# A table of ninety-two task priorities in a self-scheduled attention and gated feed-forward kernel

## Chip, cores and metric

The kernel runs on one core of a Trainium2 chip. The metric is the device time of one execution in microseconds, median of the runs. The profile describes one execution; its span, from the first to the last instruction on the core, is 276.8 us, and the run that it was taken from lasted 278.56 us.

## What is computed

Attention for 4 batches, 8 heads, 768 positions and a head dimension of 64, followed by a gated feed-forward layer over the 3072 resulting rows of width 512. Heads 0, 2 and 6 ("retrieval") attend to all earlier positions; the others attend to the first 4 positions ("sinks") and a window of 64.

```python
causal = rel >= 0
stream_keep = causal & (is_sink | ((rel >= 0) & (rel < 64)))
mask = where(is_retrieval, causal, stream_keep)
a = softmax(where(mask, q @ k.T / 8, -1e9))
x = (a @ v)                      # -> (3072, 512), heads side by side

g, val = x @ w_gate, x @ w_val   # (512, 1536) each
ffn = (gelu(g) * val) @ w_out    # (1536, 512)
out = x + sigmoid(x @ w_res) * ffn
```

## The kernel before

The Python program builds a graph of 1670 tasks (360 of them are dummy matmuls, see below), runs a list scheduler over that graph when the program is built, and emits each engine's instructions in the order that the scheduler found. On the chip nothing is scheduled any more: each engine executes its list in order and waits on semaphores where a task depends on another engine.

The 3072 rows are taken in six chunks of four tiles of 128 rows. In chunk c the tasks are, with the source line that the profile shows and the engine in brackets:

- `qkT`, `qkE`: q and k turned so that the head dimension lies on partitions (chunks 0 and 1), L631 [PE] and L646 [ACT or DVE]; later chunks use transposing DMAs, L669.
- `sc`: scores, q against k, L768 [PE]; `sk`: scores against the sinks, L856 [PE]; `exp`, L784 and L863 [ACT]; `mask`, L820 [DVE].
- `win`, `av`, `avk`: the weights times v, by window, by whole tiles and for the sinks, L885, L895, L909 [PE]; `rcp`, `norm16`, `norm`: division by the sums, L935, L946, L948 [DVE].
- `xT`, `xE`: the result turned, L963 [PE], and copied out of PSUM, L970 [ACT or DVE].
- `g`, `v`: gate and value matmuls, L988 [PE], in halves of two 512-column matmuls; there are 12 pairs f = 0..11 in a chunk. `gelu`, L1000 [ACT]; `h`, their product, L1002 [DVE].
- `res`: the residual gate, L1016 [PE], with `tanh`, L1019 [ACT]; `ff`: the output matmuls, L1031 [PE], in pieces of two; `gated` and `add`, L1035 and L1038 [DVE]; `out`, the store, L1041.
- `warm`: dummy matmuls on a blank tile, L1047 [PE], priority 1e9, so that they run when nothing else can; those that are left are dropped when the first gate matmul is placed.

Scores use half of the array's rows for each of two heads, window products half of its columns, sink scores a quarter of its rows and columns; the scheduler calls this the task's mode (`row`, `col`, `quarter`, or none for the whole array).

The part that picks the next task, with cuts:

```python
ENGS = ("pe", "act", "dve", "pool", "sp")
SWITCH = 0.1
LAT = {"pe": 0.20, "act": 0.10, "dve": 0.08, "pool": 0.12, "sp": 0.1}

def schedule(self):
    ...
    while left:
        for e in ENGS:
            if free[e] > now:
                continue
            best = bkey = None
            for t in cand[e]:
                if t.boost and all(x.end is not None and x.end <= now for x in t.boost[0]):
                    t.prio, t.boost = t.boost[1], None
                key = (int(e == "pe" and mode is not None and t.mode != mode), t.prio, t.seq)
                if t.ready > now or (best is not None and key >= bkey):
                    continue
                ...                      # a task with two possible engines; are its buffers free?
                if ok:
                    best, bkey = t, key
            ...
            dur = t.dur
            if e == "act" and t.fset and t.fset != fset:
                dur += 1.3
            if e == "pe":
                dur += SWITCH if t.mode != mode else 0.0
            free[e] = now + dur
            ...
```

So a task is a candidate once its producers are done by the scheduler's own clock. Among candidates the lowest `prio` wins, except that the tensor engine first takes one of the mode that it is in. Priorities before are given by a rule: they begin at 1000 times the chunk, with gate and value at +500, the outputs at +2400 + 10 per tile:

```python
pr = 1000 * c + 500 + f           # gate and value matmuls, gelu, product
...
if c0 == 0 and c > 0:             # their first halves are wanted late until all of xT is there
    for t in (tg, tv):
        t.boost, t.prio = ([t_ for _, t_ in xttoks], pr), 1000 * c + 1499
...
pr = 1000 * c + 2400 + 10 * lt    # res, tanh, ff, gated, add, store
...
P.pr = 1000 * c + 40 * k_         # scores of the k_-th pair of heads; sinks 1000 * c + 45
```

Two fixed order rules remain whatever the priorities are: gate and value tasks of a chunk come after all its scores (and, but for the first f, after all its `xT`), and the scores of chunk c + 1 come after the gate and value tasks of f = 10 of chunk c and after its `xT`.

PSUM has eight banks, and the kinds of task share them with caps: two score buffers of two banks each (banks 2 to 5), one pair of banks (0, 1) for the products with v, up to four banks at once out of 2 to 7 for gate and value, banks 6 and 7 for the outputs.

```python
"av2": (1, [(0, 1)]), "sc": (2, [(2, 3), (4, 5)]),
"gv": (4, one(6, 7, 5, 4, 3, 2)), "gv00": (2, one(6, 7)), "out": (2, one(6, 7)), ...
```

Of the kernel before, what the change touches and what calls it, by code (L numbers as in the profile page):

```python
# [36 lines left out]
ROWS_UNTIL = 2  # L37

VK = ((1, 4), (3, 4), (4, 5), (4, 7))

class Task:
    __slots__ = ("eng", "dur", "fn", "deps", "order", "prio", "bufs", "fset", "dma",
# [387 lines left out]
def build_kernel(nc, q, k, v, w_gate, w_val, w_out, w_res, out):  # L430
    assert N_SINK <= 64 and WINDOW == 64
    G = Graph(nc)
# [37 lines left out]
    def at(buf):  # L470
        if buf.pool is P_ps:
            return psum[:, buf.slot[0] * 512:(buf.slot[-1] + 1) * 512]
        return buf.pool.items[buf.slot]
# [68 lines left out]
    def batch(b):  # L542
        if b not in batches:
            B_ = B()
            B_.v, B_.vs, B_.vk, B_.qkt = Buf(P_v), Buf(P_vs), Buf(P_vk), Buf(P_qkt)
            B_.vtok, B_.vstok, B_.qtok, B_.ktok = {}, {}, {}, {}
            batches[b] = B_
        return batches[b]

    def values(b, a, z, base, each, on_engines=False):  # L550
# [6 lines left out]
        if a == 0:  # L557

            def vk(on, j, h0, h1):
                def fn(e):  # L560
                    o = at(BB.vk)[32 * j:32 * j + N_SINK, 2 * j:2 * j + 2, :]
                    i_ = at(BB.v)[0:N_SINK, 0, h0:h1 + 1:h1 - h0, :]
                    return e.activation(out=o, in_=i_, func=AF.Copy) if on == "act" else e.tensor_copy(out=o, in_=i_)
                return fn
            BB.vktok = [G.flex({"dve": (0.3, vk("dve", j, *hs)), "act": (0.35, vk("act", j, *hs))},
                               [BB.vtok[0]], base + 1500, bufs=[BB.v, BB.vk], name="vk") for j, hs in enumerate(VK)]
            for t in BB.vktok:
# [301 lines left out]
    def weigh(P, tiles, sinks, xbuf, x16, xtoks, xdeps, last):  # L869
# [30 lines left out]
        def sinkf(x, h):  # L900
            def fn(e):
                r = []
                for lt, (b, i) in enumerate(tiles):
# [3 lines left out]
                    j = sinks.four[b, i] if h == 4 else (1, 3, 5, 7).index(h)  # L907
                    sl = 2 * j + VK[j].index(h)
                    r.append(e.matmul(at(av)[:, o:o + 65], lhsT=at(sinks.et)[:, ko:ko + 128], rhs=at(batch(b).vk)[:, sl, :],  # L909
# [157 lines left out]
    for c in range(len(CHUNKS)):  # L1067
# [9 lines left out]
        for t in ph(c + 1, "exp"):  # L1077
            t.order += gelu[NF - 1:]

    span = G.schedule()  # L1080
    G.assign_waits()
    G.emit()
# [3 lines left out]
def bass_duo_attention_split__then__geglu_gated_residual_kernel(  # L1086
    nc: bass.Bass,
    q: bass.AP,
    k: bass.AP,
    v: bass.AP,  # L1090
    is_retrieval: bass.AP,
    n_sink: bass.AP,
    window: bass.AP,
    moe_w_gate: bass.AP,
    moe_w_val: bass.AP,
    moe_w_out: bass.AP,
    moe_w_res: bass.AP,
    out: bass.AP,
):
    assert int(n_sink) == N_SINK and int(window) == WINDOW  # L1100
    build_kernel(nc, q, k, v, moe_w_gate, moe_w_val, moe_w_out, moe_w_res, out)
# [33 lines left out]
```

The softmax here doesn't subtract the row's maximum and nothing guards it: scores larger than these inputs give would overflow.

## Time and profile before

| | before |
|---|---|
| median of 3 runs | 278.73 us (278.38 to 278.83) |
| span of the profiled execution | 276.8 us |
| PE matmul busy | 270.3 us, 98% |
| DVE, ACT, POOL busy | 143.0, 137.5, 86.2 us |
| bytes read from HBM, written | 29.36 MB, 6.29 MB |
| dummy matmuls executed (L1047) | 151, all before 22.0 us |

How to read it: matmuls overlap one another in the records. One of 512 columns is listed with 379 ns although the next may start 216 ns after it, so a busy PE is not a PE at its peak. Time that PE loses therefore shows in the distance from one matmul's start to the next one's, and in dummy matmuls, which count as busy, rather than in the busy share. In the chain of work that ended last, each row is a start, a length and a run of instructions of one line.

### The profile page before, as it was taken

To read this page: it belongs to the slowest core of one execution; us is meant where nothing else is said; L and a number is where in the kernel's file an instruction comes from. 1 tells how busy PE (TensorE), PEld (TensorE's weight loads), DVE (VectorE), ACT (ScalarE), POOL (GpSimd) and SP (SyncE) were. 2 spreads that over 40 slices of the span, in tenths; PEclk is the share of its full clock that TensorE was granted. 3 is DMA by queue.
4 is the path that set the end of the run, shared out by engine and by line. 5 is a ranking of instruction groups with operands and counts; after the bars stand their busy time and mean duration, and the time that the engine had idled before them with its cause. 6 is when DMAs were issued, how large, how long until landed. Compare 5 with 4: busy or idle time off the path is not lost.

```text
span 276.8 us, 5687 instructions
## 1 busy us (share of the span) xinstructions
PE 270.3 (98%) x2407; PEld 138.9 (50%) x2407; DVE 143.0 (52%) x260; ACT 137.5 (50%) x199; POOL 86.2 (31%) x120
## 2 busy tenths in 40 slices
PE   7999999999899999999999999999999999999995
PEld 7775454455444456444455444456444455544443
DVE  2696342477433467534377533366633258633234
ACT  3655366673433966334773333766233777333210
POOL 8999249991491613991000000000000000000000
PEclk9999999999999999999999999999999999999999
DMA  6999999999999999999711100021100011200022
GB/s 88 165 203 207 185 206 177 151 194 133 176 131 154 247 138 201 158 155 125 191 41 73 44 0 2 0 76 41 40 0 0 2 41 38 78 2 0 0 76 78
DMA packets 92474, 27.81 MB, mean 100 GB/s; under 512 B 81184, under 2 KB 88864, under 8 KB 92448
## 3 DMA queue, kind: packets, MB, share of 16 engines
q0 software_dynamic: 70320, 14.69, 66.8%
q1 hardware_dynamic: 22128, 12.76, 23.7%
q8 instruction: 19, 0.31, 0.5%
q14 instruction: 7, 0.06, 0.1%
HBM read 29.36 MB, written 6.29 MB: 129 GB/s over the span
## 4 chain that ended last, share of the span: by engine, by line
PE 95%; DVE 2%; DMA 2%; issue 1%; ACT 0%; POOLq 0%
PE ps L988 45%; PE ps L1031 23%; PE ps L1016 7%; PE ps L768 5%; PE ps L895 3%; PE ps L1047 3%; PE ps L885 2%; PE ps L963 2%; PE ps L631 2%; DMA qks<-in_q_dram 2%; PE ps L909 1%; PE ps L856 1%; ACT xT L970 0%; DVE otile L1035 0%; DVE x L946 0%
## 5 line engine op out<-in xcount | busy, mean ns | idle before, releaser
L1002 DVE SCALAR_TENSOR_TENSOR hT<-gact,ps 128x512 f16<-128x512 f16 x72 | 49.5, 687 | 70.5 <-ACT gact L1000 70.5
L988 PE MATMUL ps<-xT,wg 128*128 128x512 f16 x288 | 85.2, 379 | 0.5 <-ACT xT L970 0.5
L988 PE MATMUL ps<-xT,wv 128*128 128x512 f16 x288 | 85.2, 379 | 0.0
L1000 ACT ACTIVATE gact<-ps 128x512 f16<-128x512 f32 x72 | 43.0, 597 | 78.2 <-PE ps L988 78.2
L1031 PE MATMUL ps<-wo,hT 128*128 128x512 f16 (+1 forms) x300 | 71.6, 371 | 0.2
L988 PEld LDWEIGHTS ps<-xT,wv 128*128 128x128 f16 x288 | 28.1, 98 | 33.8
L988 PEld LDWEIGHTS ps<-xT,wg 128*128 128x128 f16 x288 | 27.7, 98 | 33.7 <-ACT xT L970 0.6
L784 ACT ACTIVATE er<-ps 128x1024 f16<-128x1024 f32 (+3 forms) x40 | 34.5, 904 | 14.4 <-PE ps L768 14.4
L1031 PEld LDWEIGHTS ps<-wo,hT 128*128 128x128 f16 x300 | 25.8, 98 | 28.4 <-DVE otile L1035 3.7
L520 POOL DMA_DIRECT2D qks<-in_k_dram x36 | 28.4, 831 | 31.8 <-DMA qkt<-qks 22.8
L1035 DVE SCALAR_TENSOR_TENSOR otile<-srs,ps 128x512 f32<-128x512 f32 (+1 forms) x25 | 16.6, 664 | 26.4 <-PE ps L1031 26.4
L520 POOL DMA_DIRECT2D qks<-in_q_dram x36 | 28.9, 851 | 0.8 <-POOLq L1117 0.8
L1016 PE MATMUL ps<-wr,xT 128*128 128x512 f16 x96 | 24.7, 380 | 0.0
L520 POOL DMA_DIRECT2D va<-in_v_dram x24 | 21.4, 943 | 6.4 <-PE ps L909 6.4
L1019 ACT ACTIVATE srs<-ps 128x512 f32<-128x512 f32 x24 | 14.4, 598 | 12.4 <-PE ps L1016 12.0
L768 PE MATMUL ps<-qkt 64*128 64x64 f16 (+4 forms) x396 | 17.2, 215 | 0.0
L1038 DVE TENSOR_TENSOR otile<-otile,xtok 128x512 f32<-128x512 f32 (+1 forms) x25 | 16.5, 661 | 0.5
L948 DVE TENSOR_TENSOR xtok<-ps,rcp 128x512 f32<-128x512 f32 x24 | 16.3, 686 | 0.3
L768 PEld LDWEIGHTS ps<-qkt 64*128 64x128 f16 x396 | 10.3, 94 | 8.2 <-issue 3.4
L784 ACT ACTIVATE es<-ps 128x1024 f16<-128x1024 f32 x12 | 12.2, 1020 | 3.5 <-PE ps L768 3.5
L1016 PEld LDWEIGHTS ps<-wr,xT 128*128 128x128 f16 x96 | 8.7, 98 | 10.4 <-ACT gact L1000 0.5
L970 ACT ACTIVATE xT<-ps 128x512 f16<-128x512 f16 x11 | 6.3, 596 | 15.2 <-PE ps L963 15.2
(58 smaller groups left out, 197.0 us busy)
## 6 DMA issues: line engine op xcount, KB each, us to landing
out_dram<-otile SPq DMA_DIRECT2D x23, 256.0 KB, 2.5
va<-in_v_dram POOLq DMA_DIRECT2D x24, 128.0 KB, 17.7
qks<-in_k_dram POOLq DMA_DIRECT2D x32, 64.0 KB, 16.3
qks<-in_q_dram POOLq DMA_DIRECT2D x32, 64.0 KB, 16.9
wg<-in_moe_w_gate_dram POOLq DMA_DIRECT2D x3, 512.0 KB, 10.0
wv<-in_moe_w_val_dram POOLq DMA_DIRECT2D x3, 512.0 KB, 12.4
wo<-in_moe_w_out_dram POOLq DMA_DIRECT2D x4, 384.0 KB, 22.4
vs<-va SPq DMA_DIRECT2D x4, 260.0 KB, 5.8
```

Of the source, the lines that this page charges most:

```text
L520: return G.add(eng, issue, lambda e: e.dma_start(out_ap(), in_ap), deps, prio, bufs=bufs, dma=cost, name=name, grp=grp)
L768: return [e.matmul(at(scr)[:, oo:oo + w], lhsT=at(BB.qkt)[half, 1, p, k0:k0 + 128], rhs=at(BB.qkt)[half, 0, p, qq:qq + w], start=True, sto ...
L784: return e.activation(out=o, in_=i_, func=AF.Exp, scale=SM_SCALE)
L948: t2 = G.add("dve", c_dve(2 * n * 64), lambda e: e.tensor_tensor(out=xview(), in0=avv(0, DHEAD), in1=scale(), op=ALU.mult), [t1] + xdeps, ...
L988: return lambda e: [e.matmul(at(dst)[:, :], lhsT=w[:, ci, f * 128:(f + 1) * 128], rhs=at(xtbuf)[:, ci, :], start=(ci == 0), stop=(ci == NC ...
L1000: ta = G.add("act", c_act(512), (lambda gb=gb, ga=ga: lambda e: e.activation(out=at(ga)[:, :], in_=at(gb)[:, :], func=AF.Gelu))(), [tg], p ...
L1002: th = G.add("dve", c_dve(512), (lambda vb=vb, ga=ga, f=f: lambda e: e.scalar_tensor_tensor(out=at(h)[:, f, :], in0=at(ga)[:, :], scalar=0 ...
L1016: e.matmul(at(rb)[:, :], lhsT=at(xtbuf)[:, ci, s], rhs=wr[:, ci, :], start=(ci == 0), stop=(ci == NCB - 1))
L1019: ta = G.add("act", c_act(512), (lambda rb=rb, sr=sr: lambda e: e.activation(out=at(sr)[:, :], in_=at(rb)[:, :], func=AF.Tanh, scale=0.5)) ...
L1031: e.matmul(at(fb)[:, w], lhsT=at(h)[:, fi, s], rhs=wo[:, fi, w], start=(fi == 0), stop=(fi == NF - 1))
L1035: t1 = G.add("dve", c_dve(n), (lambda fb=fb, sr=sr, ot=ot, w=w: lambda e: e.scalar_tensor_tensor(out=at(ot)[:, w], in0=at(sr)[:, w], scala ...
L1038: t2 = G.add("dve", c_dve(n), (lambda ot=ot, lt=lt, w=w: lambda e: e.tensor_tensor(out=at(ot)[:, w], in0=at(ot)[:, w], in1=at(xbuf)[:, lt, ...
```

## The change

A table of 92 pairs, number of a task and priority, is added, and written over the rule's priorities just before scheduling. It was found by a search over priorities. Nothing else changes: the tasks, their durations in the scheduler, their instructions, buffers, caps and order rules are the same. The purpose is another order of the tasks on the engines, and with it another choice of buffers.

```diff
+HINTS = (
+    "3:-21.19 5:-58.49 6:-58.34 403:490.65 425:595.32 427:528.41 578:-99.99 586:59.9 611:1499.22 612:516.59 "
+    "622:576.96 635:549.35 636:510.21 637:1538.66 643:580.14 647:570.57 648:558.53 649:1085.71 650:1520.19 "
... (nine more rows like these)
+    "1553:5511.01 1554:5505.99 1608:7485.06 1628:7447.37 1653:7483.11 "
+)
...
         for t in ph(c + 1, "exp"):
             t.order += gelu[NF - 1:]
 
+    for x in "".join(HINTS).split():
+        n_, p_ = x.split(":")
+        G.tasks[int(n_)].prio = float(p_)
     span = G.schedule()
```

Counted by the task that each number stands for in the list built before: 49 gate or value tasks, 12 `ff`, 7 `res`, 5 products with v, 3 `qkT`, 3 `sc`, 3 constants, 2 `xT`, 2 `tanh`, and one each of `mask`, `xE`, `norm16`, `sk`, `exp` and the activation-table task. 58 get a higher number (later), 34 a lower one (earlier). A few of them, with the rule's priority first:

| task | chunk | priority |
|---|---|---|
| 3, first constant of the causal mask [POOL] | start | -54 to -21.19 |
| 5 and 6, first two constants of the window mask [POOL] | start | -53 to -58.49, -58.34 |
| 622, `norm16` of heads 4 and 6 [DVE] | 0 | 77.5 to 576.96 |
| 635, `g0`, first half | 0 | 500 to 549.35 |
| 671, `g6`, first half | 0 | 506 to 15.77 |
| 637, `g0`, second half | 0 | 500 to 1538.66 |
| 734, `ff` of the third tile | 0 | 2420 to 1503.99 |
| 1040, `v6`, second half | 2 | 2506 to 3534.81 |
| 1608, `v10`, second half | 5 | 5510 to 7485.06 |
| 1628, `res` of the second tile | 5 | 7410 to 7447.37 |

## The prediction

> **What bounds the kernel now.** I read the page first, then the chain in order of time, then the waits. From the page:
>
> ```profile
> PE 270.3 (98%) x2407; PEld 138.9 (50%) x2407; DVE 143.0 (52%) x260; ACT 137.5 (50%) x199; POOL 86.2 (31%) x120
> ...
> PEclk9999999999999999999999999999999999999999
> ...
> PE 95%; DVE 2%; DMA 2%; issue 1%; ACT 0%; POOLq 0%
> PE ps L988 45%; PE ps L1031 23%; PE ps L1016 7%; PE ps L768 5%; PE ps L895 3%; PE ps L1047 3%; PE ps L885 2%; PE ps L963 2%; PE ps L631 2%; DMA qks<-in_q_dram 2%; PE ps L909 1%; PE ps L856 1%; ACT xT L970 0%; DVE otile L1035 0%; DVE x L946 0%
> ```
>
> PE is the bound: it has 95% of the chain, every other engine is about half idle, and the clock is full throughout. A new order takes no matmul away (apart from dummies, L1047), so it can win only what PE spends on something else. The busy share of 98% can't tell how much that is. I therefore took the distance from each matmul's start to the next one's, out of the trace.
>
> Bottom up, the dense work: gate and value, 576 matmuls at 216 ns = 124.4 us; output, 276 at 216 ns and 24 at 109 ns = 62.2 us; residual gate, 96 at 216 ns = 20.7 us. Together 207.3 us, three quarters of the span, which no order changes. The attention lines (L631, L768, L856, L885, L895, L909, L963) take 48.0 us by starts, including mode changes and waits behind them. What is lost lies in four places.
>
> The start, in the chain:
>
> ```profile
> 1.32 4.29 DMA qks<-in_q_dram
> ...
> 17.77 1.35 PE ps L1047 x21
> ...
> 20.34 0.61 ACT xT L970
> 20.99 1.18 PE ps L1047 x18
> ```
>
> The first 5.66 us pass until the first q has landed, and the program can't begin without it. From there until the first gate matmul at 22.62 us, dummies stand on the chain in ten places; they sum to 7.0 us. In that stretch PE waits for loads, for exp and masks, and for ACT and DVE between the last products and xT.
>
> Mode changes, in the chain of a later chunk:
>
> ```profile
> 216.45 0.38 PE ps L856 x4
> 216.83 0.97 PE ps L1016 x4
> ...
> 220.07 0.97 PE ps L1031 x4
> 221.04 0.86 PE ps L1016 x4
> 221.91 0.59 PE ps L768 x6
> 222.50 1.40 PE ps L1031 x6
> ```
>
> Four 512-column matmuls cost 0.86 us (221.04) where the mode stays and 0.97 us just after the sink scores (216.83). By starts, a 512-column matmul is followed after 216 ns by one of the same mode and after 309 to 312 ns by one of another; a 64-column score is followed after 29 ns or after 123 ns. So a change costs about 95 ns either way. I count 116 changes, 25 of them before 22.6 us, some 17 in each middle chunk: 116 x 0.095 = 11.0 us.
>
> Waits for another engine or a buffer on the same chain:
>
> ```profile
> 68.62 0.70 DVE x L946
> 69.45 0.40 PE ps L963 x4
> 69.88 0.61 ACT xT L970
> 70.53 19.17 PE ps L988 x88
> ```
>
> Here PE stands for normalisation and transposition at the end of chunk 1's attention: the start at 69.45 comes 0.85 us late, that at 70.53 0.63 us late. The waits of the weight loads name one that comes back, for the output banks:
>
> ```profile
> PEld ps L1031 <- DVE otile L1035: 3.7, 9, 0.5
> ```
>
> The column's 3.7 us are of weight loads, which run ahead; by starts, an output group is 0.15 to 0.18 us late behind a residual group, six times. All starts that are late by more than a mode change sum to 7.6 us, 2.4 of them before 22.6 us, so 5.2 us later.
>
> The tail: the last matmul starts at 273.43 us, and gating, adding and storing take the other 3.4 us. No priority shortens these three.
>
> **What the Trainium skill says.** "TensorEngine Tiling (Array Packing)", Key Properties, says that a change of tiling mode drains TensorE, without a figure. The trace agrees and gives one, 95 ns. "TensorE: Matmul & The Clock Gate", Back-to-back issue gap, offers two figures for 512 columns: 216 ns for a single gap and about 131 ns for a sustained stream of loads and matmuls. The trace has 216 ns in a sustained stream, so the dense 207.3 us are a floor here and hold no hidden slack. "Perfetto Trace Analysis", Identifying the Most-Contended Engine, warns that matmul busy share does not tell the distance from the bound, as seen above.
>
> **The change, part by part.** It adds and removes no instruction but dummies; its own cost on the chip is nil. 80 of the 92 numbers belong to PE tasks and 49 of these to gate and value halves. Those are the full-mode work that can be put anywhere in a chunk once xT is there, so they can fill a wait.
>
> Start. Tasks 5 and 6 (POOL, 0.35 and 0.45 us in the trace) move ahead of later loads and task 3 (0.24 us) behind them, which shifts each load by a few tenths. `norm16` of heads 4 and 6 and `xT` are put later than other work. The prize is a gate half (0.43 us) in place of the 1.18 us of dummies at 20.99, where the first two blocks of xT have just been copied. Against that, the weights must have landed: the first gate weights are issued only at 10.64 us, and the three loads of gate weights take 6.5 to 13.7 us to landing. I take off 0.8 us of the 7.0.
>
> Mode changes. The scheduler knows them (0.1 us each) and already prefers the mode that it is in, so one is left only where nothing of the same mode was ready. 52 score tasks and 18 window tasks, with two score buffers and one pair of banks for the products, can't be gathered without end: a middle chunk has five visits to scores and three to windows. One visit of scores fewer, or a score visit put right beside a window visit, saves one or two changes in a chunk. I take three per chunk off five attention phases: 15 x 0.095 = 1.4 us.
>
> Waits. Held-back halves (637, 650, 1040, and in the last chunk 1608) can be spent where an output bank or xT isn't ready: one half of 0.43 us covers any of the waits above but the two in the chain of chunk 1. I take off 1.5 of the 5.2 us.
>
> Tail. Task 1608 can stand between the residual and output groups at 263.8 and 267.5, each 0.18 us late: 0.2 us.
>
> Against these: the search knew the scheduler's clock, in which all durations are fixed. PE takes its tasks strictly in the order given. Where a producer on the chip is some tenths later than in that clock, a packed order waits and the loose one doesn't. I put 0.6 us of new waits in.
>
> Sum: -0.8 - 1.4 - 1.5 - 0.2 + 0.6 = -3.3 us. 278.73 - 3.3 = 275.4 us, 1.2% less.
>
> **The rivals.**
> 1. The gain stays in the scheduler's clock. What speaks for it: many priorities look arbitrary, as from a search that keeps whatever is a little better, and the loads take 4 to 26 us to land, which no constant describes. What speaks against it: the scheduler's 0.1 us for a change and 0.432 us for a pair of matmuls are close to the measured 0.095 and 0.431. Then 277.5 to 279 us.
> 2. The search finds much more: half of the dummies (3.5 us), a third of the changes (3.7 us) and half of the waits (2.6 us), together 9.8 us, so 269 us at best, with 272 already plausible. Against it: order rules and caps are unchanged, and the kernel's rule was already made with these in mind.
> 3. A held-back half keeps its PSUM bank. Of eight banks two serve the products; a gate half kept for a chunk's attention takes one that scores or outputs would use, and then scores wait for exp (PE behind ACT) as a new bound in these 20 us. Or the shifted constants delay masks at the start. That would cost 1 to 3 us: 277 to 281.
>
> **Range and chances.** The middle is 275.4. The upper end is rival 1 with some luck against it, 278.2; the lower one is most of what I think can be had, 272.8. Below 273.2 us it is faster by over 2%; that needs 5.6 us, more than half of rival 2, and I give it 0.16. Slower than 284.3 would need a mistake of rival 3's kind in each chunk: 0.02. The rest, 0.82, is within 2%.
>
> **What would show it.** If I am right: dummies (L1047) fall from 151 to under 140; mode changes from 116 to about 100; late starts after the start phase from 5.2 to about 4 us; the first gate matmul comes up to 1 us before 22.62; L988 appears inside the attention phases as short pieces between scores and outputs; busy times of DVE and ACT stay within 1 us. The dense 207.3 us must stay. If rival 1 holds, there are fewer changes but new "PE waits for ACT or DVE" of 0.2 to 0.5 us in the chain. If rival 3 holds, gaps before L768 released by exp or before L1031 released by gating grow. The prediction fails low if the start phase loses several us of dummies at once, which I hold back from because the loads are not mine to see; it fails high if a late load stalls an order that has nothing else left to do.

## The result, and the profile after

The kernel with the table takes 276.01 us (275.82 to 277.01) against 278.58 us for the kernel before beside it: a ratio of 0.991, with a 95% interval of 0.989 to 0.994. The prediction was 275.4 us and a range of 272.8 to 278.2.

The profiled execution spans 274.1 us, 2.7 us less than before. Lines below the table are 15 higher than in the kernel before: the gate and value matmuls are now L1003, the dummies L1062, output and residual groups L1046 and L1031, products with v L910, L900 and L924, transpositions L978.

From the page of the kernel after:

```profile
PE 267.2 (97%) x2398; PEld 138.5 (51%) x2398; DVE 139.6 (51%) x254; ACT 140.7 (51%) x205; POOL 86.2 (31%) x120
...
PE 92%; DMA 2%; POOL 2%; DVE 1%; issue 1%; ACT 1%; POOLq 0%
```

PE stays the bound, and its busy share falls although the kernel is faster: the 98% were no measure. Nine matmuls fewer (2407 to 2398) are nine dummies fewer, 151 to 142.

The chain in order of time (start, length, what) shows where the path got shorter. At the start:

```profile
20.98 0.45 PE ps L1062 x5
21.43 0.45 PE ps L978 x8
21.92 13.98 PE ps L1003 x64
```

18 dummies stood here, now 5 do, and the first gate matmul comes at 21.92 in place of 22.57 us (the chain above put it at 22.62). At the end of chunk 1's attention:

```profile
68.58 0.40 PE ps L978 x4
69.00 0.61 ACT xT L985
69.66 18.30 PE ps L1003 x84
```

The two late starts that the prediction showed here have stayed as they were, 0.85 and 0.63 us. Only the clock time of the place moved, by 0.87 us. In the last chunk:

```profile
256.72 1.73 PE ps L1031 x8
258.44 0.43 PE ps L1003 x2
258.88 5.18 PE ps L1046 x24
```

Two residual groups are taken together, then the second half of v10 (task 1608), then two output groups without a break: 24 matmuls in 5.18 us, 216 ns each. None of them starts late behind a residual group any more. In the waits of the weight loads, the row that was 3.7 us for output groups (they waited for DVE to read an output bank) has gone; what is left there of waits for DVE's `gated` (L1050) and `add` (L1053) is

```profile
PEld ps L900 <- DVE otile L1053: 0.4, 1, 0.4
...
PEld ps L1003 <- DVE otile L1050: 0.3, 1, 0.3
```

One wait is new. After the last pairs of chunk 0, the first scores of the next attention stand behind gelu and three products on DVE and start 0.2 us later than their change of mode explains:

```profile
44.42 1.97 DVE hT L1017 x3
...
46.43 0.41 PE ps L783 x16
```

The account of PE by starts, for the profiled execution of each kernel, in us. Each distance from a start to the next is put into one row, so that the rows add up to the span. Whole-array work is taken at the measured undisturbed rate (216 ns for 512 columns), a change of mode at up to 97 ns, and what is over that is a wait.

| | before | after | third bank (below) | own table of 101 (below) |
|---|---|---|---|---|
| whole-array matmuls | 222.9 | 222.9 | 222.9 | 222.9 |
| half- and quarter-array matmuls | 19.5 | 19.5 | 19.6 | 19.5 |
| dummies until first data | 4.6 | 4.6 | 4.6 | 4.7 |
| dummies later | 7.1 | 6.7 | 7.5 | 7.8 |
| changes of mode not behind a dummy (number) | 10.4 (108) | 9.6 (100) | 10.4 (108) | 10.0 (104) |
| waits on top of a change | 2.0 | 2.0 | 2.1 | 2.6 |
| other late starts | 5.0 | 3.6 | 3.6 | 2.4 |
| jitter, head and tail | 5.4 | 5.2 | 5.3 | 5.2 |
| span | 276.8 | 274.1 | 275.8 | 275.1 |

So the 2.7 us are 1.4 us of late starts, 0.8 us of mode changes, 0.4 us of dummies and 0.2 us of jitter (rounded). No work went away but nine dummies, and the one new wait of 0.2 us is small against what went. "Jitter, head and tail" is the time before the first matmul, the 3.4 us behind the start of the last one, and distances a few ns over the rate.

### The profile page after: what moved, and what is told of

The parts are those of the page before. It is cut to its first block, busy times and chain, and to the rows that moved or that the text cites. A ratio compares the mean times of both kernels' runs of the same rounds, so it can differ in the third digit from the quotient of the medians.

```text
span 274.1 us, 5645 instructions
## 1 busy us (share of the span) xinstructions
PE 267.2 (97%) x2398; PEld 138.5 (51%) x2398; DVE 139.6 (51%) x254; ACT 140.7 (51%) x205; POOL 86.2 (31%) x120
## 4 chain that ended last, share of the span: by engine, by line
PE 92%; DMA 2%; POOL 2%; DVE 1%; issue 1%; ACT 1%; POOLq 0%
PE ps L1003 45%; PE ps L1046 23%; PE ps L1031 8%; PE ps L783 5%; PE ps L910 3%; DMA va<-in_v_dram 2%; PE ps L900 2%; PE ps L978 2%; PE ps L924 2%; POOL qks L535 1%; PE ps L1062 1%; PE ps L646 1%; DVE hT L1017 1%; PE ps L871 1%; ACT xT L985 0%
## 5 line engine op out<-in xcount | busy, mean ns | idle before, releaser
L1017 DVE SCALAR_TENSOR_TENSOR hT<-gact,ps 128x512 f16<-128x512 f16 x72 | 48.7, 687 | 72.6 <-ACT gact L1015 48.2
L1015 ACT ACTIVATE gact<-ps 128x512 f16<-128x512 f32 x72 | 42.8, 597 | 72.0 <-PE ps L1003 65.9
L1003 PE MATMUL ps<-xT,wg 128*128 128x512 f16 x288 | 78.6, 380 | 0.5 <-ACT xT L985 0.5
L1003 PE MATMUL ps<-xT,wv 128*128 128x512 f16 x288 | 78.8, 379 | 0.0
L1046 PE MATMUL ps<-wo,hT 128*128 128x512 f16 (+1 forms) x300 | 70.4, 371 | 0.0
L1003 PEld LDWEIGHTS ps<-xT,wg 128*128 128x128 f16 x288 | 27.7, 98 | 33.7 <-ACT xT L985 0.6
L1003 PEld LDWEIGHTS ps<-xT,wv 128*128 128x128 f16 x288 | 27.9, 98 | 33.4 <-DVE hT L1017 0.4
L1046 PEld LDWEIGHTS ps<-wo,hT 128*128 128x128 f16 x300 | 27.0, 98 | 27.5 <-issue 1.5
L1050 DVE SCALAR_TENSOR_TENSOR otile<-srs,ps 128x512 f32<-128x512 f32 (+1 forms) x25 | 16.5, 661 | 24.2 <-PE ps L1046 24.1
L1031 PE MATMUL ps<-wr,xT 128*128 128x512 f16 x96 | 24.6, 380 | 0.0
L535 POOL DMA_DIRECT2D va<-in_v_dram x24 | 21.3, 940 | 6.6 <-PE ps L924 6.6
L1053 DVE TENSOR_TENSOR otile<-otile,xtok 128x512 f32<-128x512 f32 (+1 forms) x25 | 16.6, 665 | 0.6
L1031 PEld LDWEIGHTS ps<-wr,xT 128*128 128x128 f16 x96 | 8.4, 98 | 9.9 <-issue 0.7
```

The source lines that it names most:

```text
L535: return G.add(eng, issue, lambda e: e.dma_start(out_ap(), in_ap), deps, prio, bufs=bufs, dma=cost, name=name, grp=grp)
L1003: return lambda e: [e.matmul(at(dst)[:, :], lhsT=w[:, ci, f * 128:(f + 1) * 128], rhs=at(xtbuf)[:, ci, :], start=(ci == 0), stop=(ci == NC ...
L1015: ta = G.add("act", c_act(512), (lambda gb=gb, ga=ga: lambda e: e.activation(out=at(ga)[:, :], in_=at(gb)[:, :], func=AF.Gelu))(), [tg], p ...
L1017: th = G.add("dve", c_dve(512), (lambda vb=vb, ga=ga, f=f: lambda e: e.scalar_tensor_tensor(out=at(h)[:, f, :], in0=at(ga)[:, :], scalar=0 ...
L1031: e.matmul(at(rb)[:, :], lhsT=at(xtbuf)[:, ci, s], rhs=wr[:, ci, :], start=(ci == 0), stop=(ci == NCB - 1))
L1046: e.matmul(at(fb)[:, w], lhsT=at(h)[:, fi, s], rhs=wo[:, fi, w], start=(fi == 0), stop=(fi == NF - 1))
```

## The experiments

### Parts of the table

The question was whether the table is a sum of savings, each with its entries, or one order that hangs together. First the start alone:

```diff
-HINTS: 92 entries
+HINTS: the 11 entries with numbers up to 622
```

> Only the 11 entries of the table that belong to the start (constants, transpositions, scores, masks, xT and normalisation of chunk 0) are kept; all other priorities are the rule's. Theory A, the table is a sum of parts that each bring their own saving: the first gate matmul starts near 21.9 us as with the whole table, and the 0.65 us carry through to the end: about 278.0 us. Theory B, the entries only work together, each tuned to the order that the others make: the gain of the start is lost again later, and the time is within 0.3 us of before.

Measured: 278.88 us, ratio 1.000 (0.9995 to 1.001). The saving at the start is there and gone again: the first gate matmul comes at 22.09 us, 0.48 us earlier than before, and later dummies take 6.5 in place of 7.1 us. But waits on top of mode changes rise from 2.0 to 2.7 us and other late starts from 5.0 to 5.4 us. Most of it stands in one place, the end of chunk 1's attention: a transposition at 64.48 us and a window product at 65.67 us wait for DVE, 0.76 and 0.64 us, and the main gate run behind them starts at 70.76 us, later than the 70.53 us of before. Theory B.

```diff
-HINTS: 92 entries
+HINTS: the 21 entries of res, tanh and ff tasks
```

> Only the 21 entries for the residual gate, tanh and output matmuls are kept. Theory A (sum of parts): the six late output groups behind a residual group, 1.0 us in all, go, as they went with the whole table: about 277.5 us. Theory B (whole only): without the gate and value entries that stand in for them these groups come at other times, new late starts appear, and it is no faster than before, perhaps 1 us slower (278.5 to 280).

Measured: 279.84 us, ratio 1.0045 (1.003 to 1.006): slower than before. The waits of PE's matmuls in this run have a row that the kernel before hadn't:

```profile
PE ps L1038 <- DVE otile L1042: 1.2, 4, 0.4
```

L1038 are the output matmuls here, L1042 reads their bank. They still wait for it, and longer. The waits on top of mode changes are 4.0 us in place of 2.0; some 0.7 us of the rise is another wait, of a window product for DVE. Theory B again. The same 21 entries belong to an order in which these waits vanish.

```diff
-"... 653:525.88 654:576.91 655:1026.63 ..."
+"... 653:525.88 655:1026.63 ..."
```

> The whole table without one of its 92 entries, number 654 (a first half of v3 in chunk 0, 503 by the rule, 576.91 by the table). Theory A: one entry out of 92 is worth a few hundredths of a us, so about 276.0 us. Theory B: v3 then goes before v6 and v7, its PSUM banks and those of the pairs begun early hold each other up in chunk 0, and dummies come back in numbers: slower than before, by 2 to 8 us, with over 200 dummies in the trace.

Measured: 288.38 us, ratio 1.034 (1.029 to 1.040). One number out of 92 left out costs 12 us against the whole table, and makes the kernel 9.7 us slower than it was without any, more than the 2 to 8 us of theory B. No other entry was left out alone. The chain of this run in chunk 0:

```profile
44.49 1.73 PE ps L1003 x8
46.22 2.35 PE ps L1062 x42
48.57 3.47 PE ps L1003 x16
...
55.20 1.28 ACT L799
...
56.49 1.02 ACT er L799
...
57.52 1.28 ACT L1015
```

There are 287 dummies; those after the first data take 15.9 us against 6.7 us with the whole table, and the other late starts 6.7 against 3.6 us. The two rows of 1.28 us are loads of the activation table: an exp of the next chunk now stands between two gelus of this one, and the table is loaded for it and again for the gelu. Of the 12.0 us between the two spans, dummies are 9.1 and late starts 3.1 (1.4 of these at half of the clock behind a wait, see the last section).

The profile doesn't show PSUM banks, but the scheduler's list for this kernel has them, in its own clock. v3, no longer held back, is placed at 23.8 us and takes bank 6. Its gate g3, which the table puts late, is placed only from 49.0 to 50.7 us, and until both are multiplied the bank stays taken. v4 holds bank 7 in the same way until g4 at 43.0 us. The pair f = 0 of chunk 0 may use banks 6 and 7 alone, so g0 is placed only at 54.2 us. Dummies are dropped when g0 is placed (the program asks for f = 0, not for any gate matmul), so until then they fill each wait. With the whole table v3 is placed at 42.8 us, after both halves of g3. So this order suffers from halves that keep their banks, as in the prediction's third rival, though here they hold up another gate pair and not scores.

If entries hang together, do later ones hang on earlier ones only? Two runs cut the table from behind.

```diff
-HINTS: 92 entries
+HINTS: the first 54 (start, chunks 0 and 1); in the other run, the first 84 (all but the last chunk)
```

> The table's first 54 entries: start, chunk 0 and chunk 1. The scheduler works forward, so leaving out later entries should leave the order up to there nearly as with the whole table. Theory (an entry depends on those before it, not on those after it): the saving that the whole table had made by the end of chunk 1's attention (its main gate run starts at 69.66 in place of 70.53 us) is kept, and the rest of the program takes its old time: 277.6 to 278.0 us. Rival (the parts all depend on one another, later on earlier and earlier on later): no faster than before, as with the 11 and the 21 entries.

> The table without the 8 entries of the last chunk. By the same theory it loses only what those 8 do at the end, at most the two or three late output groups there (0.18 us each) and a mode change or two: 276.2 to 276.7 us. Rival: one entry missing was enough to lose 12 us in chunk 0, so eight missing bring it back to 278.7 or more.

Measured: 278.03 us, ratio 0.9975 (0.9966 to 0.9985), and 276.41 us, ratio 0.992 (0.990 to 0.993). With the first 54, the main gate run of chunk 1 starts nearly as early as with the whole table (69.66 us):

```profile
69.77 18.30 PE ps L998 x84
```

So the table can be shortened from its end, and what is lost is about what the dropped entries had brought: 0.7 us come from the first 54, some 1.6 more from the 30 of chunks 2 to 4, and the last 8 bring too little to be told apart. The cut can't be made anywhere: the first 11 alone brought nothing.

That the entries hang together is a property of the scheduler's choices and not of the chip. By its own clock the list ends at 274.4 us before and at 271.2 us with the table; at 274.3 us with the 11 entries, 275.3 with the 21, 281.5 without entry 654, 273.2 with the first 54 and 271.7 with the first 84. Against before this is -0.1, +0.9, +7.1, -1.2 and -2.7 us, where the chip had +0.2, +1.1, +9.7, -0.8 and -2.4.

### The output banks

```diff
-        ... "out": (2, one(6, 7)), ...
+        ... "out": (3, one(6, 7, 1)), ...
```

> The kernel before, no table, with a third PSUM bank for the outputs: cap 3, banks 6, 7 or 1 in place of cap 2, banks 6 or 7. Theory: the six late starts of an output group behind a residual group (1.03 us by starts) wait for an output bank to be read. With a third bank they go without any table: about 277.5 us, and down to 276.8 if later waits go too. Rival: these starts wait for the residual gate's own reader or for weights; then they stay and the time is that of before, or more, since bank 1 is also half of the pair for the products with v.

Measured: 277.20 us, ratio 0.995 (0.993 to 0.996), without any table. The six late starts behind residual groups, 1.03 us before, are down to one of 0.08 us. In the tail, the second and third output groups took 2.76 us in the kernel before; now each takes what twelve matmuls need, 2.59 us. In the chain of before and then of this run:

```profile
263.81 2.76 PE ps L1031 x12
```

```profile
263.17 2.59 PE ps L1031 x12
```

These waits were waits for an output bank to be read. A seventh, of 0.30 us at 144.98 us, where an output group stood behind DVE's reading of the bank and not behind a residual group, has gone with them, here and with the table. One line of the caps removes the waits that the table removes by another order of residual and output groups, and over half as much as the table gains (1.5 of 2.6 us by the medians; the profiled execution, 277.57 us, gains 1.0) comes from that line alone.

### What a change of mode costs

```diff
+extra = lambda e: [e.matmul(at(dst)[:, 0:64], lhsT=blank[:, :], rhs=blank[:, 0:64], start=True, stop=True)]
                                  # control; ahead of the first half of each gate pair
+extra = lambda e: [e.matmul(at(dst)[:, 0:64], lhsT=blank[0:64, :], rhs=blank[0:64, 0:64], start=True, stop=True)]
                                  # half of the rows: a change of mode and back
```

> Control for the next run. The kernel before, with one extra matmul of 64 columns on the blank tile, whole array, ahead of each of the 72 gate pairs; it writes into the bank that the pair's first matmul overwrites. By the 29 ns from start to start of a 64-column matmul, 72 x 0.029 = 2.1 us more: about 280.8 us.

> The same 72 extra matmuls, but on half of the array's rows, so that each brings a change of mode and a change back, 144 more changes than the control. Theory (a change costs PE 95 ns on the path, whatever stands around it): 144 x 0.095 = 13.7 us more than the control, about 294.5 us, and start-to-start distances of about 311 and 123 ns in place of 216 and 29. Rival (the 95 ns seen before are the wait for other engines that such places happen to have): within 2 us of the control.

Measured: 280.82 us for the control and 295.40 us with the changes. The trace has 258 changes against the control's 116, 142 more and not 144, since two of the extra matmuls stand where the mode changed anyway. The difference of 14.58 us over 142 changes is 103 ns for one. By starts, the extra matmul follows a 512-column one after 312 in place of 216 ns, and is followed after 132 in place of 28 ns. In the chain of the control and then of the other run, the extra matmul (L988) between gate matmuls:

```profile
76.36 0.03 PE ps L988
```

```profile
77.40 0.13 PE ps L988
```

A change costs the path about 0.1 us in the middle of dense work too, and the rival (waits that such places happen to have) is out, so the 8 changes that the table saved outside the dummies are its 0.8 us.

### Can another order do better?

The same priorities were searched again, longer, with the scheduler's clock as the only judge. That gave two tables whose span by that clock is 269.5 us each, against 271.2 us for the table under study.

```diff
-HINTS: 92 entries
+HINTS: 88 other entries; in the other run, 101
```

> Another table of 88 entries, from a longer search of my own over the same priorities, judged by the scheduler's clock alone. Theory (that clock describes PE's order well enough for what it saves to be saved on the chip): it takes off more than the table under study, about 274.5 us. Rival (a still tighter order waits on the chip for producers that come some tenths later than planned): no better than 276 us, with late starts above the 2.8 us of the table under study.

> A second table, of 101 entries, from an independent search of the same kind that ended at the same length by the scheduler's clock, but with more dummies and fewer mode changes. Theory: within 0.5 us of the other one, about 274.5 us, though the losses are shared out otherwise. Rival: the two differ by 1 us or more, since each order meets the chip's delays by chance.

Measured: 279.27 us (278.44 to 282.86), ratio 1.004 (1.002 to 1.006), and 276.44 us, ratio 0.992 (0.990 to 0.994). The further gain by the scheduler's clock didn't reach the chip: one table is slower than no table, the other no better than the one under study, and the two differ by 2.8 us, as both rivals said. The 101 had the fewest late starts of the kernels so far, and two of them are most of its loss. The chain around the first:

```profile
12.51 13.20 DMA wv<-in_moe_w_val_dram
...
25.75 4.27 PE ps L1003 x19
```

Value weights, issued at 12.51, were on chip 13.2 us later, and the next matmul in PE's list needed them. It starts 1.4 us late. The other late start, 0.9 us at 61.33, ends a line of DVE instructions. The execution of the 88 that was profiled is the longest of its 20 (seven took 281.3 to 282.9 us, the others 278.4 to 279.9), so its waits may be larger than usual; the chain shows their kind:

```profile
47.09 21.34 DMA qks<-in_q_dram
...
68.44 2.25 SPq L685
...
71.39 9.31 DMA out_dram<-otile
...
80.73 0.70 DVE otile L1051
...
81.47 4.56 PE ps L1004 x14
```

A load of q takes 21.3 us; a transposing DMA on SP waits for it (L685); a store stands behind it in SP's list; the store's tile comes free only when that has landed; DVE waits for the tile, and PE for the PSUM bank that DVE should have read. In the scheduler's clock each of these transfers has a length worked out from fixed numbers. The next runs put later transfers into that clock and searched a third table for it.

```diff
     def schedule(self):
         for t in self.tasks:
+            if t.dma:
+                t.late += {"vs": 3.0, "dT": 1.5, "ld": 0.0 if t.prio < -30 else 1.2}.get(t.name, 0.0)
+                t.dur += 0.6 if t.name == "dT" else 0.0
```

> A third table of my own, of 109 entries, found against a scheduler's clock with three numbers changed, since the two before had waited on the chip for loads and for the stores and transposes behind them: shifted copies of v land 3.0 us later than assumed, transposing DMAs take 0.6 us longer to issue and land 1.5 us later, loads after the first ones land 1.2 us later. Theory (what those two tables lost on the chip was lost to transfers that the scheduler thought earlier than they are): no wait of PE for a transfer over 0.5 us, and about 273 to 274.5 us. Rival (any order packed tighter than the one under study loses it again, whatever the clock): 276 us or more.

> Control: the same three numbers changed in the scheduler's clock, with the rule's priorities and no table. If the later loads alone made the gain, this one is faster than before too. I expect no gain, within 1 us of before: 278.5 to 280 us.

Measured: 276.56 us, ratio 0.993 (0.991 to 0.995), with the table of 109 entries, and 285.26 us, ratio 1.024 (1.022 to 1.026), with the rule. The expectation for the table was wrong by 2 us, as its rival said, and that for the control by 5 us. The table's waits of PE for transfers are short in the profiled execution, though one is over the 0.5 us that were expected at most:

```profile
PE ps L788 <- DMA qkt<-qks: 0.7, 1, 0.7
PE ps L1051 <- DMA wo<-in_moe_w_out_dram: 0.4, 1, 0.4
```

Its late starts outside mode changes are down to 2.0 us from 5.0. But it pays in other rows of the account: dummies after the first data 7.9 us where the table under study has 6.7, changes 10.0 against 9.6, waits on top of changes 2.5 against 2.0. The eight runs range from 275.76 to 278.46 us; whether its transfers landed otherwise in the longer ones is not shown, since one execution was profiled. In the control, waits on top of mode changes take 6.8 us and other late starts 6.5. The longest, 2.9 us, ends the same kind of chain as with the 88:

```profile
80.92 16.91 DMA qks<-in_k_dram
...
99.07 1.27 SPq L672
...
101.66 5.22 DMA out_dram<-otile
...
107.65 1.89 PE ps L1019 x4
```

A load of k takes 16.9 us, transposing DMAs in SP's list wait for it, a store behind them lands late and keeps its tile, and a residual group (L1019) waits for the bank that DVE then reads. By its changed clock the scheduler ends this list at 277.3 us, 3.0 us more than before; on the chip it is 6.6 us more. Against the control the table saves 8.7 us, against the kernel before 2.1. No version that was run is faster than the kernel after. The third output bank together with a table was not run.

## Why the prediction was right, and where it was off

**The bound** held: whole-array work (the prediction's dense 207.3 us and the whole-array part of attention) is 222.9 us in each column of the account, and what was gained or lost was in the four places named.

**Waits**, 1.5 us taken off: of the late starts of 5.2 us after the start phase, 3.9 are left by the same count, 1.3 us less. The six at the output bank went, 1.03 us, as named, and the 0.30 us at 144.98 with them; the two of chunk 1 did not, which the prediction had said. The third-bank run shows the cause, an output bank still to be read.

**Mode changes**, 1.4 us taken off: this term was mis-sized. The cost of one was right (95 ns read, 103 ns measured with 142 added), the number was not: 116 fell to 109 and not to 101, about half of the saving.

**Start**, 0.8 us taken off: the first gate matmul came 0.65 us earlier and dummies fell from 151 to 142, not under 140, which is 0.4 us of them. The first gate work is that of f = 7 and f = 6, put first by the table. The run with the 11 start entries shows what the prediction had no term for: such a saving does not carry through by itself.

**Tail**, 0.2 us: task 1608 stands between residual and output groups, and the late groups there are gone. They are two of the six above, so the prediction counted them twice. The last chunk's eight entries together are too small to tell in the time.

**New waits**, 0.6 us put on: 0.2 us were seen, at 46.43 us. The savings in start, mode changes and tail were put too high, the new waits too; these errors cancelled in part, and that 275.4 came within 0.6 us of 276.0 is in part luck.

**Signs.** Late starts came out as expected; dummies, mode changes and the busy times did not. DVE went from 143.0 to 139.6 us and ACT from 137.5 to 140.7 where both were to stay within 1 us: six small instructions, four of them casts of x, went from DVE to ACT, since the scheduler gives such a task to the engine that would end it first. Neither bounds the kernel. The prediction's 80 entries of PE tasks are 82 by the list of the change.

**Rivals.** The first (a gain that stays in the scheduler's clock) did not hold for this table, which gains 3.2 us by that clock and 2.6 on the chip; it did for the one of 88, and for what the one of 101 should have gained beyond it. The second (twice the gain) was not reached here, nor by three longer searches. The third (held-back halves) holds in part for a table one entry short, where the bank is kept from a gate pair. What the prediction missed altogether is that the entries are no sum: it added up savings by place, which was right for the finished order and for cuts from its end, and wrong for the other parts that were run.

## What to carry to other kernels

Where an engine is at its bound, do the account by starts first: what an order can win is dummies, mode changes and late starts, and here that was some 25 us, of which the table found a tenth. Before a table of tuned numbers, look for the resource behind a wait that comes back: one more output bank in the caps gave over half as much and can be explained. A table of priorities for a list scheduler names tasks by their place in the list and was found for one graph; one number left out cost 12 us. No changed graph was run with it, but it is safer to search again after each change. The scheduler's clock tells the large losses before a run, as it did for that number; the last microseconds must be measured, since the chip's transfers do not keep to that clock.

## What the runs showed of the hardware

A change of the array's mode costs 0.10 us even between dense matmuls (142 changes, 14.6 us).

From one matmul's start to the next, 4.2 us passed before 81.47 us in the run of the 88, 3.5 us before 59.47 in the run without entry 654, and 3.0 us before 107.65 in the control with later transfers. Behind each the clock granted to PE fell and 512-column matmuls started 427 ns apart, as in the four of 1.89 us at 107.65 above, which take 0.86 us elsewhere. The mean granted clock was 0.58 from 59.4 to 63.0 us and 0.56 from 107.6 to 111.0 us; for the 88 it was 0.69 over the stretch below. Behind 2.7 us (before 61.98 in the run of the 88) and 1.6 us (before 25.75 in that of the 101) it stayed full. The columns are the stretch, its length, busy time and number of instructions for PE, weight loads, DVE, ACT and POOL, the granted clock, the DMA share and GB/s:

```profile
81.40:86.00 4.60, 4.53 (x15) 1.82 (x16) 2.59 (x5) 0.60 (x1) 4.60 (x7) 0.69 1.81 153
```

So each of these three waits cost PE more than its own length: in the run of the 88 the seven starts that follow are late by 1.4 us in all.
